# VectorE takes over one head of a third pair in 22 of 32 blocks of attention A

## The chip, the cores and the metric

The kernel runs as one program on one core of a Trainium2 chip. The metric is the device time of one execution in microseconds (us). The core has five engines with a queue each, and each works its queue strictly in order: TensorE (PE, with its weight loads shown as PEld), VectorE (DVE), ScalarE (ACT), GpSimd (POOL) and SyncE (SP), which here issues most transfers. They wait for one another through semaphores.

## The reference

Two independent attention problems over 2048 tokens and 576 features with 32 heads of 18 features, whose outputs stand side by side:

```python
# A: 32 query heads share one key head and one value head
q = (x @ wq).reshape(B, S, H, Dh).transpose(0, 2, 1, 3);  k = x @ wk;  v = x @ wv
p = softmax(einsum("bhqd,bkd->bhqk", q, k) * Dh ** -0.5)
a = einsum("bhqk,bkd->bhqd", p, v).transpose(0, 2, 1, 3).reshape(B, S, H * Dh) @ wo

# B: four segments of 512 tokens; in each, causal-like attention plus a memory of the segments before
logits = einsum("bhqd,bhkd->bhqk", qs, ks) * scale + mask
o = g * (phi(qs) @ M / den) + (1 - g) * (softmax(logits) @ vs)
M, z = M + phi(ks).T @ vs, z + phi(ks).sum()
```

What the change touches is A: for each head, 2048 x 2048 exponentials of scores, and their product with the values.

## The kernel before

**Stages.** In the first 290 us or so the projections, the key and value stacks and the bounds are made. Then comes the main stage, and at the end a last projection.

**Blocks.** The main stage is a list of blocks. A block of A is (c, hg): 512 queries (c = 0 to 3) and four heads (hg = 0 to 7), 32 blocks in all. Between them stand 32 small blocks of B, by a fixed list (`after`, line 874), mostly in pairs; from the fourth quarter of A on there are none left.

**Items.** A block of A has 16 key tiles `kt` of 128 keys. For each there are two items, `pr` 0 and 1, of two heads each: an item is one tile `E` of scores in PSUM, 128 keys x 2 heads x 512 queries. Its exponentials go to a tile `P` in SBUF, and `P` is multiplied with the values into `O`.

**Turns.** The program is written out in turns of three items. A block of A has 32 items, so eleven turns, 0 to 10, of which the last has two; a block of B has two turns. In turn k, TensorE makes the three `E` of this turn (line 924; line 932 for B), then one step of the output projection of an earlier quarter as "fill" (`F`, line 778; line 834 in the early blocks), then the products (`O`, line 972) that belong two turns back. ScalarE takes the exponentials (line 942) of the first and third item straight from PSUM. The middle item is first copied by VectorE to a tile `W` (line 939), which frees its PSUM early, and ScalarE takes it last. There are three tiles `E`, so each item of a turn waits for its counterpart of the turn before to be read: two for ScalarE, the middle one for VectorE's copy.

**The heads on VectorE.** For two items of each block of A, named in `BY_DVE` as (kt, pr), VectorE computes the exponentials of one of the two heads itself, and ScalarE only does the other: (0, 1) in turn 0 and (5, 0) in turn 3. Such a tile is named `PD` (two buffers). `exponentials` (line 896) first scales the scores from PSUM (line 900), and queues three pairs of operations, lines 902 and 903, 904 and 905, 906 and 907. One pair is worked off in each following turn (`slow`), behind this turn's copy. `copied` marks the middle item, so the copy to `W` shrinks to half where the item is also such an item.

**Positions of the products.** `turn_of` gives for each `pr` the order in which the key tiles are multiplied: the natural order, but the two tiles of `BY_DVE` are taken out and put in again at the positions `LATE` (7 and 12), since they are ready later.

**Other work on VectorE.** It copies finished `O` (line 981) and `F` (line 802) out of PSUM, and takes the reciprocals of the softmax sums (line 729): a large one for heads 0 to 27 of a quarter and a small one for heads 28 to 31. GpSimd multiplies finished heads with those inverses (line 762, "weighs"), behind the VectorE work of the same turn and only in a turn in which no pair is queued. In ten of the 32 blocks it does so.

The orders of TensorE, ScalarE and VectorE are as written in the program; those of GpSimd and SyncE are set by a scheduler.

Of the kernel before, what the change touches and what calls it, by code (L numbers as in the profile page):

```python
# [24 lines left out]
NKT = S // 128  # L25
# [26 lines left out]
POLY = [1.0925606709321247, 32.334180715292455, 88.7610992882796, 4291.093056129828]  # L52
MANTISSA, ONE_BITS, EXPONENT = 0x7FFFFF, 0x3F800000, 0xFF800000

BY_DVE = ((0, 1), (5, 0))
LATE = (7, 12)
QALL = [(slice(0, 36, 2), 0), (slice(1, 36, 2), 1), (slice(36, 54), 0)]
CA = 618
MZ = 126 + 32
# [15 lines left out]
def attention_pair_kernel(ctx, tc, a_xT, a_w, a_wo, b_xT, b_w, b_wo, b_beta, ident_d, hmask_d, bmask_d, cmask_d, sel_d, zmask_d, selx_d, sely_d, out):  # L75
# [534 lines left out]
    with tc.If(loose > 0, preferred_fallthrough_block=False):  # L610
        with ExitStack() as ph:
# [37 lines left out]
            with tc.For_i(0, H, 1) as h:  # L649
                qs = pq.tile([128, S], F32R, name="gq")  # L650
                load_rows(qs, qB, h, QALL)
                ks = pq.tile([128, S], F32R, name="gk")
                load_rows(ks, kB, h, KROWS)
                mc = pq.tile([128, 16], F32, name="gmc")
                for i in range(NKT):
                    s, j = divmod(i, 4)
                    n = 128 * (j + 1)
# [238 lines left out]
    def exponentials(p, e, whole):  # L896

        u, w = (pp.tile([128, 512], F32, name=nm, bufs=1) for nm in "nq")
        v, stt, y = nc.vector, nc.vector.scalar_tensor_tensor, p.bitcast(U32)
        v.tensor_scalar(y, e, EXP_A, EXP_B, op0=ALU.mult, op1=ALU.add)  # L900
        ops = [
            lambda: v.tensor_scalar(u.bitcast(U32), y, MANTISSA, ONE_BITS, op0=ALU.bitwise_and, op1=ALU.bitwise_or),
            lambda: v.tensor_scalar(w.bitcast(U32), y, EXPONENT, None, op0=ALU.bitwise_and),
            lambda: stt(p, u, POLY[0], u, op0=ALU.add, op1=ALU.mult),
            lambda: stt(p, p, POLY[1], u, op0=ALU.add, op1=ALU.mult),
            lambda: stt(p, p, POLY[2], p, op0=ALU.add, op1=ALU.mult),
            lambda: stt(p, p, POLY[3], w, op0=ALU.add, op1=ALU.mult),  # L907
        ]
        slow.extend((now[0] + 2 + i, p, ops[2 * i : 2 * i + 2], whole) for i in range(3))

    def scores(it, pr, copied):

        ab, c, hg, kt = it
        st = stacks[ab, c, hg // 2]
        h = 2 * (hg % 2) + pr
        e = psE.tile([128, 2, 512], F32, name="E")
        dve = ab == "A" and (kt, pr) in BY_DVE
        p = pp.tile([128, 2, 512], F32, name="PD" if dve else "P", bufs=2 if dve else PBUFS)
        state[it, pr] = p
        n = 512 if ab == "A" else 512 - 128 * kt if kt < 2 else 384  # L920
        if ab == "A":
            for j, r0 in enumerate(HALF):
                rows = slice(r0, r0 + KR)
                nc.tensor.matmul(e[:, j], kstA[rows, 128 * kt : 128 * kt + 128], st[rows, h, :], start=True, stop=True)  # L924
            if dve:
                exponentials(p[:, 0], e[:, 0], p)
        else:
            for k, c0 in BKEYS[kt]:
                ks = slice(128 * k, 128 * k + 128)
                for j, r0 in enumerate(HALF):  # L930
                    rows = slice(r0, r0 + KR)
                    nc.tensor.matmul(  # L932
                        e[:, j, c0 : c0 + 512 - 128 * k], st[rows, 4 + h, ks], st[rows, h, 128 * k :], start=True, stop=True
                    )
        src, hs = e, slice(0, 2)
        if copied:
            src = pp.tile([128, 2, 512], F32, name="W", bufs=2)
            hs = slice(1, 2) if dve else slice(0, 2)
            gate.append(nc.vector.tensor_copy(src[:, hs, :n], e[:, hs, :n]))  # L939

        def exponential():
            nc.scalar.activation(p[:, hs, :n], src[:, hs, :n], AF.Exp, scale=SCALE)  # L942
            if ab == "B":

                m = len(BKEYS[kt])
                diag = p.rearrange("p a (b t) -> p a b t", t=256)[:, :, 0:m, 0:128]
                nc.gpsimd.affine_select(  # L947
                    diag, diag, pattern=[[0, 2], [0, m], [1, 128]], base=0, channel_multiplier=-1, compare_op=ALU.is_ge, fill=0.0
                )

        return exponential
# [3 lines left out]
    def products(b, m, hf):  # L955


        ab, c, hg = b
        if m == hf == 0:
            acc[0] = psO.tile([128, C], F32, name="O")  # L960
        o = acc[0]
        last = (NKT - 1 if ab == "A" else 2) == m
        for j in range(4):
            kt = turn_of[j // 2][m] if ab == "A" else m
            p = state[b + (kt,), j // 2]
            assert all(x[3] is not p for x in slow)
            k, p0, q0, n = (kt, 256 * hf, 256 * hf, 256) if ab == "A" else BHALF[kt][hf]
            if ab == "A":
                v = VA[:, VW * kt : VW * kt + 32]
            else:  # L970
                v = vseg[c][:, k, VW * (4 * hg + j) : VW * (4 * hg + j) + 32]
            nc.tensor.matmul(  # L972
                o[32 * j : 32 * j + 32, q0 : q0 + n],
                v,
                p[:, j % 2, p0 : p0 + n],
                start=m == hf == 0,
                stop=last and hf == 1,
            )
        if last and hf:
            osb = pa.tile([128, C], F32, name="oe", bufs=4)  # L980
            nc.vector.tensor_copy(osb, o)  # L981
            od = oA if ab == "A" else oB
            nc.sync.dma_start(od[c][4 * hg : 4 * hg + 4].rearrange("h r t -> (h r) t"), osb)
            return hg
        return None


    turn_of = []
    for pr in range(2):
        ks = [kt for kt in range(NKT) if (kt, pr) not in BY_DVE]  # L990
        for (kt, p_), pos in zip(BY_DVE, LATE):
            if p_ == pr:
                ks.insert(pos, kt)
        turn_of.append(ks)

    keys = {ab: list(dict.fromkeys((ab, c, hg // 2) for a_, c, hg in blocks if a_ == ab)) for ab in "AB"}

# [94 lines left out]
    with tc.manual_schedule(engines={ENG.PE, ENG.Activation, ENG.DVE}):  # L1092
# [23 lines left out]
        for k in range(len(turns) + 2):  # L1116
            now[0] = k
            exps = [scores(its[n], pr, i == 1) for i, (n, pr) in enumerate(turns[k])] if k < len(turns) else []
            for i in (0, 2, 1) if len(exps) == 3 else range(len(exps)):
                exps[i]()  # L1120
# [148 lines left out]
```

## Time and profile before

| what | value |
|---|---|
| median of 3 runs | 1415.69 us (1415.11 to 1416.66) |
| the profiled execution's own time | 1417.1 us |
| its span, first to last instruction | 1415.4 us |
| granted TensorE clock, mean | 0.997 |
| main stage | from about 291 us to about 1376 us of the span |
| a block of A that follows a block of A, fourth quarter | 28.74 to 28.77 us |

The page gives for each engine the share of the span in which it is busy, and groups instructions by line, with the tile written and the tile read (`P<-E`). In the timeline every row is a start time, a duration, an engine, a line and a count of like instructions in a row; in square brackets stands how long the engine idled before it and what ended the wait. The duration of a ScalarE or VectorE row runs into the next row's start, since neighbours overlap; the distance from start to start tells what one instruction takes out of the engine's time. A view by windows gives, for stretches from one time to another, the length and the busy time of each engine in them. Cut at the starts of the `E` matmuls, such stretches are the turns.

### The profile page before, as it was taken

To read this page: it belongs to the slowest core of one execution; us is meant where nothing else is said; L and a number is where in the kernel's file an instruction comes from. 1 tells how busy PE (TensorE), PEld (TensorE's weight loads), DVE (VectorE), ACT (ScalarE), POOL (GpSimd) and SP (SyncE) were. 2 spreads that over 40 slices of the span, in tenths; PEclk is the share of its full clock that TensorE was granted. 3 is DMA by queue.
4 is the path that set the end of the run, shared out by engine and by line. 5 is a ranking of instruction groups with operands and counts; after the bars stand their busy time and mean duration, and the time that the engine had idled before them with its cause. 6 is when DMAs were issued, how large, how long until landed. Compare 5 with 4: busy or idle time off the path is not lost.

```text
span 1415.4 us, 40396 instructions
## 1 busy us (share of the span) xinstructions
PE 1397.0 (99%) x17132; PEld 843.5 (60%) x17132; DVE 976.6 (69%) x1413; ACT 1205.9 (85%) x1479; POOL 230.5 (16%) x326
## 2 busy tenths in 40 slices
PE   9999999989999999999999999999999999999998
PEld 6788888745554555555555555555555555555558
DVE  6656456466687767777777777766768777777763
ACT  4543434479999999999999999999999999999991
POOL 2431000003312310402110122113010320001002
PEclk9999999999999999999999999999999999999999
DMA  9766547466675445332312442232103321110013
GB/s 281 257 217 188 167 141 223 165 173 202 170 214 166 125 138 166 99 116 85 111 58 70 147 147 58 91 114 83 50 35 101 100 75 47 36 58 18 18 59 112
DMA packets 90723, 172.66 MB, mean 122 GB/s; under 512 B 14576, under 2 KB 22889, under 8 KB 90110
## 3 DMA queue, kind: packets, MB, share of 16 engines
q1 hardware_dynamic: 84122, 160.01, 36.8%
q0 software_dynamic: 1664, 4.78, 1.3%
q10 hardware_dynamic: 4752, 5.24, 1.1%
q8 instruction: 136, 2.23, 0.7%
q14 instruction: 49, 0.40, 0.1%
HBM read 99.32 MB, written 70.67 MB: 120 GB/s over the span
## 4 chain that ended last, share of the span: by engine, by line
PE 70%; ACT 4%; DMA 2%; DVE 2%; issue 1%; SPq 0%; ACTq 0%; DVEq 0%
PE O L972 32%; PE E L924 20%; PE F L778 11%; ACT P L942 4%; PE E L932 3%; PE E L1170 2%; DVE W L939 1%; PE F L834 1%; DMA vseg<-vB 0%; DMA stB<-qB 0%; DVE sm L729 0%; DMA woA<-a_wo 0%; DMA oA<-oe 0%; PE F L1170 0%; PE O L1170 0%
## 5 line engine op out<-in xcount | busy, mean ns | idle before, releaser
L942 ACT ACTIVATE P<-E 128x1024 f32<-128x1024 f32 (+1 forms) x800 | 804.8, 1116 | 3.1 <-PE E L924 2.9
L939 DVE COPY W<-E 128x1024 f32<-128x1024 f32 (+2 forms) x416 | 465.8, 1120 | 217.7 <-PE E L924 155.7
L972 PE MATMUL O<-P,VA 128*32 128x256 f32 x7680 | 508.1, 380 | 0.0
L942 ACT ACTIVATE P<-W 128x1024 f32<-128x1024 f32 (+1 forms) x352 | 410.4, 1166 | 5.3 <-DVE W L939 5.3
L972 PEld LDWEIGHTS O<-P,VA 128*32 128x32 f32 x7680 | 260.0, 110 | 139.1 <-issue 6.6
L924 PE MATMUL E<-stA,kstA 56*128 56x512 f32 x1920 | 321.6, 433 | 3.0 <-DVE W L939 2.0
L924 PEld LDWEIGHTS E<-stA,kstA 56*128 56x128 f32 x1920 | 154.9, 184 | 169.3 <-ACT P L942 77.8
L947 POOL TENSOR_SCALAR_AFFINE_SELECT P<-P 128x256 f32<-128x256 f32 (+1 forms) x192 | 94.5, 493 | 420.3 <-ACT P L942 381.8
L762 POOL TENSOR_TENSOR o<-o,rb 126x512 f32<-126x512 f32 (+1 forms) x55 | 72.6, 1350 | 480.4 <-DVE PD L907 377.3
L778 PE MATMUL F<-woB,o 126*32 126x192 f32 (+1 forms) x1920 | 127.0, 338 | 0.8 <-DVE osb L802 0.8
L778 PEld LDWEIGHTS F<-woB,o 126*32 126x32 f32 (+1 forms) x1920 | 38.5, 108 | 72.6 <-issue 66.7
L972 PE MATMUL O<-P,vseg 128*32 128x256 f32 (+2 forms) x1536 | 81.7, 344 | 0.0
L981 DVE COPY oe<-O 128x512 f32<-128x512 f32 x64 | 44.3, 692 | 42.0 <-PE O L972 41.1
L252 PE MATMUL pj<-xh,wBl 128*126 128x512 f32 x180 | 72.4, 403 | 0.0
L121 ACT CAST qp<-pj 126x512 fp32r<-126x512 f32 (+1 forms) x54 | 30.9, 585 | 48.2 <-DVE kmB L450 33.5
L252 PE MATMUL pj<-xh,wBh 128*126 128x512 f32 x180 | 71.8, 400 | 0.0
L972 PE MATMUL O<-PD,VA 128*32 128x256 f32 x512 | 71.8, 379 | 0.0
L932 PE MATMUL E<-stB 56*128 56x256 f32 (+3 forms) x512 | 62.4, 348 | 1.6 <-ACT P L942 0.9
L778 PE MATMUL F<-woA,o 126*32 126x192 f32 (+1 forms) x960 | 63.9, 338 | 0.0
L972 PEld LDWEIGHTS O<-P,vseg 128*32 128x32 f32 x1536 | 49.0, 109 | 24.5 <-issue 2.0
L900 DVE TENSOR_SCALAR PD<-E 128x512 uint32<-128x512 f32 x64 | 44.2, 691 | 27.3 <-PE E L924 26.5
L122 DVE TENSOR_TENSOR qp<-pj,qp 126x512 fp32r<-126x512 f32 (+1 forms) x54 | 36.7, 686 | 35.4 <-ACT qp L121 35.2
(195 smaller groups left out, 1485.0 us busy)
## 6 DMA issues: line engine op xcount, KB each, us to landing
stB<-kB SPq DMA_DIRECT2D x96, 144.0 KB
stB<-qB SPq DMA_DIRECT2D x32, 288.0 KB
stA<-qA SPq DMA_DIRECT2D x30, 288.0 KB
oA<-oe SPq DMA_DIRECT2D x32, 256.0 KB
oB<-oe SPq DMA_DIRECT2D x32, 256.0 KB
qA<-qp SPq DMA_DIRECT2D x16, 504.0 KB
kB<-qp SPq DMA_DIRECT2D x16, 504.0 KB
qB<-qp SPq DMA_DIRECT2D x16, 504.0 KB
```

The lines of the kernel that those rows point to most:

```text
L122: hold(nc.vector.tensor_tensor(qp[:R, 1, :n], src, qp[:R, 0, :n].bitcast(F32), op=ALU.subtract))
L252: nc.tensor.matmul(dst, w[:, c0 : c0 + M], x, start=i == 0, stop=i == len(ops) - 1)
L762: ins = tc.keep_in_program_order(nc.gpsimd.tensor_tensor(dst, a, b, op=op))
L778: nc.tensor.matmul(dst[32 * j : 32 * j + 32], parts[ab, c][: RT[t], t, r0 : r0 + 32], wo[ab][: RT[t], t, c0 : c0 + n], start=start, stop=stop,
L900: v.tensor_scalar(y, e, EXP_A, EXP_B, op0=ALU.mult, op1=ALU.add)
L924: nc.tensor.matmul(e[:, j], kstA[rows, 128 * kt : 128 * kt + 128], st[rows, h, :], start=True, stop=True)
L932: nc.tensor.matmul(e[:, j, c0 : c0 + 512 - 128 * k], st[rows, 4 + h, ks], st[rows, h, 128 * k :], start=True, stop=True)
L939: gate.append(nc.vector.tensor_copy(src[:, hs, :n], e[:, hs, :n]))
L942: nc.scalar.activation(p[:, hs, :n], src[:, hs, :n], AF.Exp, scale=SCALE)
L947: nc.gpsimd.affine_select(diag, diag, pattern=[[0, 2], [0, m], [1, 128]], base=0, channel_multiplier=-1, compare_op=ALU.is_ge, fill=0.0)
L972: nc.tensor.matmul(o[32 * j : 32 * j + 32, q0 : q0 + n], v, p[:, j % 2, p0 : p0 + n], start=m == hf == 0, stop=last and hf == 1,)
L981: nc.vector.tensor_copy(osb, o)
```

## The change

A third item, (9, 1), joins the table, in turn 6, but only in the blocks of A that are not in a new set `WEIGHED`: the ten blocks in which GpSimd weighs heads. So 22 blocks have three such items and ten have two. The table now holds the positions too: (0, 1) is multiplied at position 5, before at 7; (5, 0) stays at 12; (9, 1) stands at position 15, the last. `turn_of` becomes a function of the block.

```diff
-BY_DVE = ((0, 1), (5, 0))
-LATE = (7, 12)
+BY_DVE = {(0, 1): 5, (5, 0): 12, (9, 1): 15}
+WEIGHED = {(0, 3), (0, 6), (0, 7), (1, 1), (1, 6), (1, 7), (2, 2), (2, 6), (2, 7), (3, 4)}
...
-        dve = ab == "A" and (kt, pr) in BY_DVE
+        dve = ab == "A" and (kt, pr) in by_dve(c, hg)
         p = pp.tile([128, 2, 512], F32, name="PD" if dve else "P", bufs=2 if dve else PBUFS)
...
-            kt = turn_of[j // 2][m] if ab == "A" else m
+            kt = turn_of(c, hg)[j // 2][m] if ab == "A" else m
...
+    def by_dve(c, hg):
+
+        return [x for n, x in enumerate(BY_DVE) if n < 2 or (c, hg) not in WEIGHED]
+
+    def turn_of(c, hg):
+
+        order = []
+        for pr in range(2):
+            ks = [kt for kt in range(NKT) if (kt, pr) not in by_dve(c, hg)]
+            for kt, p_ in by_dve(c, hg):
+                if p_ == pr:
+                    ks.insert(BY_DVE[kt, p_], kt)
+            order.append(ks)
+        return order
```

VectorE's queue in block (3, 1) before, from the second pair of (5, 0) in turn 5 on; the copies belong to turns 6, 7, 8, 9 and 10:

```order
L904 SCALAR_TENSOR_TENSOR PD<-n 128x512
L905 SCALAR_TENSOR_TENSOR PD<-PD,n 128x512
L939 COPY W<-E 128x1024
L906 SCALAR_TENSOR_TENSOR PD<-PD 128x512
L907 SCALAR_TENSOR_TENSOR PD<-PD,q 128x512
L939 COPY W<-E 128x1024 x3
L802 COPY osb<-F 128x192
L939 COPY W<-E 128x1024
```

and with the change, from turn 6 on:

```order
L900 TENSOR_SCALAR PD<-E 128x512
L939 COPY W<-E 128x512
L906 SCALAR_TENSOR_TENSOR PD<-PD 128x512
L907 SCALAR_TENSOR_TENSOR PD<-PD,q 128x512
L939 COPY W<-E 128x1024
L902 TENSOR_SCALAR n<-PD 128x512
L903 TENSOR_SCALAR q<-PD 128x512
L939 COPY W<-E 128x1024
L904 SCALAR_TENSOR_TENSOR PD<-n 128x512
L905 SCALAR_TENSOR_TENSOR PD<-PD,n 128x512
L939 COPY W<-E 128x1024
L802 COPY osb<-F 128x192
```

The whole copy of turn 6 has become a scaling and a half copy, and a pair stands behind the copy of each of the turns 7, 8 and 9 (the last of the three pairs follows the row shown last).

VectorE's queue in block (0, 5), one of the three blocks of A (hg = 5 in quarters 0 to 2) in which the largest reciprocal is taken, before, from the copy of turn 6 on:

```order
L939 COPY W<-E 128x1024
L802 COPY osb<-F 128x192
L906 SCALAR_TENSOR_TENSOR PD<-PD 128x512
L907 SCALAR_TENSOR_TENSOR PD<-PD,q 128x512
L729 RECIPROCAL sm_6557<-sm_6557 112x256
L732 TENSOR_SCALAR sm_6557<-sm_6557,omg 112x128
L939 COPY W<-E 128x1024 x3
L729 RECIPROCAL sm_6638<-sm_6638 128x32
```

and with the change, from the reciprocal on:

```order
L729 RECIPROCAL sm_6593<-sm_6593 112x256
L732 TENSOR_SCALAR sm_6593<-sm_6593,omg 112x128
L939 COPY W<-E 128x1024
L902 TENSOR_SCALAR n<-PD 128x512
L903 TENSOR_SCALAR q<-PD 128x512
L939 COPY W<-E 128x1024
L904 SCALAR_TENSOR_TENSOR PD<-n 128x512
L905 SCALAR_TENSOR_TENSOR PD<-PD,n 128x512
L939 COPY W<-E 128x1024
L906 SCALAR_TENSOR_TENSOR PD<-PD 128x512
L907 SCALAR_TENSOR_TENSOR PD<-PD,q 128x512
L729 RECIPROCAL sm_6674<-sm_6674 128x32
```

The three pairs stand between the two reciprocals, where there were only copies.

TensorE's queue in block (3, 1) before, turns 5 and 6 (`E` scores, `F` fill, `O` products; `PD` where the product reads a tile with a head from VectorE):

```order
L924 MATMUL E<-stA,kstA 128x512 x6
L778 MATMUL F<-woA,o 32x192 x4
L972 MATMUL O<-P,VA 32x256 x12
L924 MATMUL E<-stA,kstA 128x512 x6
L778 MATMUL F<-woA,o 32x192 x4
L972 MATMUL O<-P,VA 32x256 x10
L972 MATMUL O<-PD,VA 32x256 x2
```

and with the change:

```order
L924 MATMUL E<-stA,kstA 128x512 x6
L778 MATMUL F<-woA,o 32x192 x4
L972 MATMUL O<-P,VA 32x256 x6
L972 MATMUL O<-PD,VA 32x256 x2
L972 MATMUL O<-P,VA 32x256 x2
L972 MATMUL O<-PD,VA 32x256 x2
L924 MATMUL E<-stA,kstA 128x512 x6
L778 MATMUL F<-woA,o 32x192 x4
L972 MATMUL O<-P,VA 32x256 x12
```

The product of (0, 1) has moved from turns 6 and 7 into turn 5, all of it ahead of the `E` of turn 6. The number of matmuls in a turn is the same.

More of the change, by code (lines that the diff above doesn't have):

```diff
@@ L985, in products @@
         return None
[L988 to L994, printed above, removed]
+    def by_dve(c, hg):
[9 more added lines that the diff above has]
+        return order
     keys = {ab: list(dict.fromkeys((ab, c, hg // 2) for a_, c, hg in blocks if a_ == ab)) for ab in "AB"}
```

## The prediction

> **What bounds the kernel now.** I read the page first, then the main stage turn by turn.
>
> ```profile
> PE 1397.0 (99%) x17132; PEld 843.5 (60%) x17132; DVE 976.6 (69%) x1413; ACT 1205.9 (85%) x1479; POOL 230.5 (16%) x326
> ACT  4543434479999999999999999999999999999991
> ```
>
> TensorE reads 99% busy, but ScalarE is at nine tenths or more in every slice of the main stage too. Both cannot be told apart from shares, so I cut one block of A that follows a block of A, (3, 1), at the starts of its `E` matmuls. Each row is a turn: its length, then busy time by engine. These are turns 0, 1, 7, 8, 9 and 10, and the sum of all eleven.
>
> ```profile
> 1168.82:1171.04 2.22, 2.22 (x34) 1.16 (x30) 1.44 (x3) 2.22 (x3) 0.00 (x0) 1.00 0.02 7
> 1171.04:1173.82 2.78, 2.78 (x44) 1.43 (x40) 1.74 (x3) 2.78 (x5) 0.00 (x0) 1.00 0.00 0
> ...
> 1187.06:1189.71 2.65, 2.65 (x43) 1.42 (x39) 1.93 (x3) 2.65 (x4) 0.00 (x0) 1.00 0.00 0
> 1189.71:1192.38 2.67, 2.67 (x42) 1.42 (x38) 1.23 (x1) 2.67 (x4) 0.00 (x0) 1.00 0.00 0
> 1192.38:1195.16 2.78, 2.78 (x42) 1.42 (x38) 1.49 (x2) 2.78 (x4) 0.00 (x0) 1.00 0.00 0
> 1195.16:1197.58 2.42, 2.42 (x42) 1.24 (x38) 1.23 (x1) 2.42 (x4) 0.00 (x0) 1.00 0.55 159
> sum 28.76, PE 28.76 PEld 15.18 DVE 21.32 ACT 28.76 POOL 0.00; mean PE 2.61 PEld 1.38 DVE 1.94 ACT 2.61 POOL 0.00
> ```
>
> Turns of the same matmuls take 2.65 us in the middle of the block and 2.78 at turns 1 and 9. (Turn 0 has fewer products, turn 10 fewer scores.) ScalarE has no idle time in any of them. What differs is who makes TensorE wait:
>
> ```profile
> 1187.06 0.56 PEld L924 LDWEIGHTS E<-stA,kstA 56*128 56x128 f32 x6 [0.41 <-issue]
> ...
> 1192.98 0.19 PEld L924 LDWEIGHTS E<-stA,kstA 56*128 56x128 f32 x2 [0.30 <-ACT P L942]
> ```
>
> In turn 7 TensorE loads its six weights in one go; in turn 9 the last two stand 0.30 us until ScalarE has read the third `E` of the turn before. So 2.65 is TensorE's own pace, and 2.78 is ScalarE's. ScalarE's pace shows in the timeline of (3, 0):
>
> ```profile
> 1148.65 2.08 ACT L942 ACTIVATE P<-E 128x1024 f32<-128x1024 f32 x2
> 1150.45 0.79 ACT L942 ACTIVATE PD<-W 128x512 f32<-128x512 f32 x1
> 1150.98 2.10 ACT L942 ACTIVATE P<-E 128x1024 f32<-128x1024 f32 x2
> ...
> 1153.75 2.10 ACT L942 ACTIVATE P<-E 128x1024 f32<-128x1024 f32 x2
> ```
>
> From start to start, a turn with a half item takes it 1150.98 - 1148.65 = 2.33 us, a full turn 1153.75 - 1150.98 = 2.77. It loses 0.12 on TensorE in every full turn, wins it back in turns 0, 3 and 10, and by turn 8 its delay reaches TensorE. Over a block the two engines are nearly level: ScalarE needs all of 28.76 us, TensorE 2.22 + 2.42 + 9 x 2.65 = 28.49.
>
> **ScalarE's half.** In 22 blocks a whole item of turn 6 becomes a half: 2.77 - 2.33 = 0.44 us less ScalarE work each. TensorE's pace caps what of it is seen. From turn 7 on the delay is 0.44 smaller, more than the 0.02, 0.13 and 0.13 by which turns 8, 9 and the next block's turn 1 exceed 2.65, so all three go: 0.28 per block. ScalarE then has 28.32 us of work against 28.49 and idles. Nine of the 22 blocks are followed by another block of A and meet no large reciprocal; the sum of eight of them stands here, and the last block of A is the ninth.
>
> ```profile
> sum 229.87, PE 229.87 PEld 121.94 DVE 172.08 ACT 229.81 POOL 2.49; mean PE 28.73 PEld 15.24 DVE 21.51 ACT 28.73 POOL 0.31
> ```
>
> 9 x 0.28 = 2.5 us; bounds 0 (the 2.78s are something else) and 9 x 0.44 = 4.0 (TensorE could go faster).
>
> Seven more blocks are followed by a pair of blocks of B. There the delay is also seen in B's second turn:
>
> ```profile
> 940.06:942.86 2.80, 2.80 (x47) 1.65 (x43) 0.96 (x1) 2.80 (x5) 1.49 (x4) 1.00 0.01 3
> ...
> 940.50 0.53 PEld L932 LDWEIGHTS E<-stB 56*128 56x128 f32 x8 [0.25 <-ACT P L942]
> ```
>
> The 0.15 of turns 8 and 9 goes as before. Of the 0.25 here I take 0.21: with the whole 0.44 gone, ScalarE would be ahead of VectorE's copy of turn 10 and wait for that instead. 7 x 0.36 = 2.5, bounds 7 x 0.15 = 1.05 and 7 x 0.40 = 2.8.
>
> The first block, (0, 0), has no fill. These are the starts of turns 5, 6, 8 and 9:
>
> ```profile
> 305.19 0.96 PE L924 MATMUL E<-st,kstA 56*128 56x512 f32 x6
> 307.52 1.21 PE L924 MATMUL E<-st,kstA 56*128 56x512 f32 x6
> ...
> 312.87 0.72 PE L924 MATMUL E<-st,kstA 56*128 56x512 f32 x4
> ...
> 315.64 0.72 PE L924 MATMUL E<-st,kstA 56*128 56x512 f32 x4
> ```
>
> TensorE can do a turn there in 2.33 and is held at 2.77, so all 0.44 counts (bounds 0 and 0.44). In (0, 1) and (0, 2) the fill is wider (line 834) and I credit nothing, 0.44 each at most.
>
> **VectorE's side.** What its operations take:
>
> ```profile
> 1148.49 0.69 DVE L900 TENSOR_SCALAR PD<-E 128x512 uint32<-128x512 f32 x1
> 1149.10 0.68 DVE L939 COPY W<-E 128x512 f32<-128x512 f32 x1
> 1149.70 0.68 DVE L906 SCALAR_TENSOR_TENSOR PD<-PD 128x512 f32<-128x512 f32 x1
> 1150.41 0.69 DVE L907 SCALAR_TENSOR_TENSOR PD<-PD,q 128x512 f32<-128x512 f32 x1
> 1151.21 1.23 DVE L939 COPY W<-E 128x1024 f32<-128x1024 f32 x1
> 1152.36 0.42 DVE L902 TENSOR_SCALAR n<-PD 128x512 uint32<-128x512 uint32 x1
> 1152.69 0.42 DVE L903 TENSOR_SCALAR q<-PD 128x512 uint32<-128x512 uint32 x1
> ...
> 1155.00 0.35 DVE L802 COPY osb<-F 128x192 f32<-128x192 f32 x1
> 1155.27 0.68 DVE L904 SCALAR_TENSOR_TENSOR PD<-n 128x512 f32<-128x512 f32 x1
> 1155.98 0.69 DVE L905 SCALAR_TENSOR_TENSOR PD<-PD,n 128x512 f32<-128x512 f32 x1
> 1156.60 1.22 DVE L939 COPY W<-E 128x1024 f32<-128x1024 f32 x1
> ...
> 1161.80 1.23 DVE L939 COPY W<-E 128x1024 f32<-128x1024 f32 x1 [1.42 <-PE E L924]
> ```
>
> By starts: scaling 0.61, half copy 0.60, whole copy 1.15, first pair 0.33 + 0.42 = 0.75, second 0.71 + 0.62 = 1.33, third 0.71 + 0.69 = 1.40. Turn 6 was 1.15 + 1.40 = 2.55 and becomes 0.61 + 0.60 + 1.40 = 2.61; turns 7, 8 and 9 were a copy alone (the 1.42 idle ahead of turn 8's) and become 1.90, 2.48 and 2.55. That is 3.54 us more per block, 78 us in all, and every turn still ends inside 2.65. The cover is that idle time. Where an evacuation (0.27) joins turn 9, the next copy is 2.82 - 2.65 = 0.17 late. ScalarE takes that copy last in its turn, and the 0.17 us it idles per block after the change (28.49 - 28.32) pay for it. So nothing in ordinary blocks; bounds 0 and 0.17 x 16 = 2.7.
>
> A rule of the Trainium skill (VectorE: DVE Perf Modes, section "The DRAIN you can't avoid") speaks against this: the next operation starts only when the pipeline of the one before is empty. By it turns 6 and 9 would cost their full durations, 2.74 and 2.60, with an evacuation 2.95, and some 0.15 more per ordinary block would come off, 2.4 us in all, leaving 1.2 of the gain. The rows disagree: the operation behind the half copy starts 0.60 after it though it lasts 0.68.
>
> Where a large reciprocal stands in the queue, the idle time is already used up (block (0, 5)):
>
> ```profile
> 533.26 1.75 DVE L729 RECIPROCAL sm<-sm 112x256 f32<-112x256 f32 x1
> ...
> 535.24 2.35 DVE L939 COPY W<-E 128x1024 f32<-128x1024 f32 x2
> ...
> 536.51 0.50 PE L924 MATMUL E<-stA,kstA 56*128 56x512 f32 x2 [0.54 <-DVE W L939]
> ```
>
> Here turn 7's copy already waits for the reciprocal and TensorE for the copy. ScalarE idles too, so its 0.44 buys nothing. Turn 6's extra 0.06 lengthens that wait. Behind it, turn 8's copy moves by the first pair, 0.75, and turn 10's by what the idle time no longer absorbs, about half a microsecond, of which I let 0.2 reach TensorE. So 3 blocks x 0.25 = 0.75 lost; bounds 3 x 0.06 and 3 x 1.40, the last pair in full.
>
> Block (0, 2) has smaller reciprocals but the wide fill, whose evacuations (line 839) load VectorE as well:
>
> ```profile
> 413.90 1.23 DVE L939 COPY W<-E 128x1024 f32<-128x1024 f32 x1 [1.63 <-PE E L924]
> 415.04 0.74 DVE L839 TENSOR_SCALAR o<-F,gt 126x512 f32<-126x512 f32 x1
> 415.70 0.24 DVE L729 RECIPROCAL sm<-sm 128x16 f32<-128x16 f32 x1
> ```
>
> Turns 7 to 9 get 0.75 + 1.33 + 1.40 = 3.48 against 1.63 of idle time ahead of turn 9's copy and 0.4 or so behind it: turn 10's copy comes about 1.3 late, and I book 1.1 (bounds 0.4 and 1.4).
>
> **Costed at nothing.** The product of (0, 1) moves from turns 6 and 7 to 5; its last pair is done in turn 3, and it must be out before the scaling of (9, 1) takes its buffer in turn 6, which it is by a whole `E` group. Its tiles 9 to 15 are multiplied one position earlier; the tightest, ScalarE's last item of a turn, is read second in the next turn's products, as other tiles are already before. The stores of the small inverses on SP's queue move behind one or two loads in four places; their readers are issued turns later. GpSimd's queue keeps its order, and the weighing blocks get no third head.
>
> **The sum.** Gains 2.5 + 2.5 + 0.44 = 5.4; costs 0.75 + 1.1 = 1.85; net 3.6 us. The profiled execution took 1417.1 (span 1415.4) and would take 1413.5; the median of the runs is 1.4 below it, so I forecast 1412.1, 0.25% less. A measurement tells about 0.2%, 2.8 us, from no change.
>
> **Rivals.** *The bubbles stay.* Turn 1 and B's second turn follow a short turn 0, and a short turn may simply be less than one round trip from `E` through ScalarE back to TensorE, whatever the delay. For it: both follow the 2.22 turn. Against: ScalarE has no idle time there. Then only turns 8 and 9 give, 16 x 0.15 = 2.4, plus 0.44, less 1.85: 1.0 us, 1414.7.
>
> *VectorE ends last* (slower). Place: the copies of turns 8 to 10. It decides once a copy stands more than the 0.17 a block can spare behind. For it: four turns in a row now fill 2.48 to 2.61 of 2.65. Against: turn 6 is 2.55 before and does not hold TensorE up. If pairs took 0.3 more each, turns 8 and 9 would be 2.78 and 2.85 where they were 2.67 and 2.78: 0.18 x 16 blocks = 2.9, plus 1.85 and no gain: 1420.
>
> *ScalarE alone is the bound.* If TensorE's 2.65 were not its floor, the whole 22 x 0.44 = 9.7 would go: 1406. For it: ScalarE never idles. Against: turn 7, where TensorE does not wait, is no shorter than 2.65. The Trainium skill (Perfetto Trace Analysis, section "Identifying the Most-Contended Engine") says to disregard matmul busy time and to take the busiest of the others, which by the page's 85% is ScalarE; that is this rival.
>
> **Chances and range.** Forecast 0.60, bubbles stay 0.25, VectorE last 0.11, ScalarE alone 0.04. The net of the forecast spreads from 2 to 6 us by its bounds, about five in six of it above 2.8. Faster by over 0.2%: 0.50 + 0.04 = 0.54; within: 0.10 + 0.25 = 0.35; slower: 0.11. The range goes from all gains without costs (5.9 with B's upper bound, 1409.7, and a little for (0, 1)) to just above no change: 1409.2 to 1416.5; the forecast's own is 1409.7 to 1413.7.
>
> **What would show it.** Turns 8 and 9 at 2.65 in the 16 ordinary blocks, turn 1 near 2.65, idle time on ScalarE once per block, VectorE busy some 78 us more, longer waits for line 939 in the hg = 5 blocks. Turns of 2.8 from turn 8 on with waits for line 939 everywhere would make it wrong, as would a turn 1 still at 2.78.

## The result, and the profile after

| | median of the runs | ratio to before, 95% interval | (0, 1) to (3, 7), us |
|---|---|---|---|
| before | 1415.71 us (22 runs) | | 1001.79 |
| changed | 1412.83 us (22 runs) | 0.9983 [0.9977, 0.9990] | 998.79 |

The changed kernel is 0.17% faster, 2.4 us by the ratio; 1412.1 was forecast. The last column is the stretch of the profiled execution from the first scores of block (0, 1) to those of the last block, (3, 7). It leaves out two places that differ between executions of one kernel, and will serve as the finer measure. One run of those told below, with a half left out, took 1890.48 us at a granted clock of 0.654, and its ratio does not count it.

From the page of the changed kernel, busy time and ScalarE's slices:

```profile
PE 1393.8 (99%) x17132; PEld 846.7 (60%) x17132; DVE 1046.6 (74%) x1567; ACT 1198.1 (85%) x1479; POOL 230.1 (16%) x326
ACT  4543434479999999999999999999999999999991
```

VectorE has 70.0 us more to do (976.6 before), ScalarE 7.8 less (1205.9 before). Block (3, 1) by turns (length, then busy time of PE, PEld, DVE and ACT), turns 0, 1, 8, 9 and 10 and the sum:

```profile
1167.15:1169.37 2.22, 2.22 (x34) 1.16 (x30) 1.45 (x3) 2.22 (x3) 0.00 (x0) 1.00 0.07 26
1169.37:1172.03 2.66, 2.66 (x44) 1.43 (x40) 1.73 (x3) 2.66 (x5) 0.00 (x0) 1.00 0.00 0
...
1187.92:1190.56 2.64, 2.64 (x42) 1.42 (x38) 1.89 (x3) 2.64 (x4) 0.00 (x0) 1.00 0.00 0
1190.56:1193.21 2.65, 2.65 (x42) 1.42 (x39) 2.52 (x5) 2.65 (x5) 0.00 (x0) 1.00 0.03 6
1193.21:1195.62 2.41, 2.41 (x40) 1.24 (x36) 2.11 (x3) 2.27 (x4) 0.00 (x0) 1.00 0.56 159
sum 28.47, PE 28.47 PEld 15.21 DVE 24.55 ACT 28.33 POOL 0.00; mean PE 2.59 PEld 1.38 DVE 2.23 ACT 2.58 POOL 0.00
```

Turns 1 and 9 have gone from 2.78 to 2.66 and 2.65: the block lasts as long as TensorE needs, and ScalarE idles 0.14 us in turn 10. What it waits for there is seen in VectorE's queue from turn 9 into the next block, and in ScalarE's:

```profile
1191.40 1.23 DVE L939 COPY W<-E 128x1024 f32<-128x1024 f32 x1
1192.54 0.35 DVE L802 COPY osb<-F 128x192 f32<-128x192 f32 x1
1192.81 0.68 DVE L906 SCALAR_TENSOR_TENSOR PD<-PD 128x512 f32<-128x512 f32 x1
1193.52 0.69 DVE L907 SCALAR_TENSOR_TENSOR PD<-PD,q 128x512 f32<-128x512 f32 x1
1194.13 1.22 DVE L939 COPY W<-E 128x1024 f32<-128x1024 f32 x1
1196.39 0.69 DVE L900 TENSOR_SCALAR PD<-E 128x512 uint32<-128x512 f32 x1 [1.04 <-PE E L924]
```

```profile
1194.15 1.10 ACT L942 ACTIVATE P<-E 128x1024 f32<-128x1024 f32 x1
1195.38 1.06 ACT L942 ACTIVATE P<-W 128x1024 f32<-128x1024 f32 x1
```

VectorE works without a gap from turn 9 into turn 10. The copy ends at 1194.13 + 1.22 = 1195.35, and ScalarE takes it at 1195.38, with nothing to do in between. So VectorE, though idle 1.04 us right behind, is at that one place already last.

Where the change costs, in (0, 2), the same queue runs past the end of the block:

```profile
415.95 0.68 DVE L906 SCALAR_TENSOR_TENSOR PD<-PD 128x512 f32<-128x512 f32 x1
416.66 0.69 DVE L907 SCALAR_TENSOR_TENSOR PD<-PD,q 128x512 f32<-128x512 f32 x1
417.27 0.25 DVE L729 RECIPROCAL sm<-sm 128x16 f32<-128x16 f32 x1
417.55 0.24 DVE L732 TENSOR_SCALAR sm<-sm,omg 128x16 f32<-128x16 f32 x1
417.70 1.22 DVE L939 COPY W<-E 128x1024 f32<-128x1024 f32 x1
```

```profile
418.97 0.19 PEld L932 LDWEIGHTS E<-stB 56*128 56x128 f32 x2 [0.36 <-DVE W L939]
```

The copy of turn 10 ends 0.6 us into block B (1, 0); TensorE waits for it and, later in that block, for ScalarE. The block of B lasts 5.40 us where it lasted 4.46. In (0, 5), behind the large reciprocal, TensorE waits longer for the copy than before (0.54):

```profile
537.04 0.49 PE L924 MATMUL E<-stA,kstA 56*128 56x512 f32 x2 [0.78 <-DVE W L939]
```

But it only comes to this wait sooner. From the start of the block the wait ends after 537.04 - 514.74 = 22.30 us, before after 536.51 - 514.18 = 22.33, and turn 8 takes 3.70 in both.

### The profile page after: what moved, and what is told of

Same layout as the page of the kernel before. It is cut to its first block, busy times and chain, and to the rows that moved or that the text cites. A ratio compares the mean times of both kernels' runs of the same rounds, so it can differ in the third digit from the quotient of the medians.

```text
span 1411.0 us, 40566 instructions
## 1 busy us (share of the span) xinstructions
PE 1393.8 (99%) x17132; PEld 846.7 (60%) x17132; DVE 1046.6 (74%) x1567; ACT 1198.1 (85%) x1479; POOL 230.1 (16%) x326
## 4 chain that ended last, share of the span: by engine, by line
PE 71%; ACT 4%; DVE 2%; issue 1%; DMA 1%; SPq 0%; POOL 0%; ACTq 0%
PE O L972 33%; PE E L924 20%; PE F L778 11%; ACT P L942 4%; PE E L932 3%; PE E L1178 2%; DVE W L939 1%; PE F L834 1%; DMA vseg<-vB 0%; DVE sm L729 0%; DMA woA<-a_wo 0%; PE F L1178 0%; PE O L1178 0%; DVE o L839 0%; DVE oe L981 0%
## 5 line engine op out<-in xcount | busy, mean ns | idle before, releaser
L942 ACT ACTIVATE P<-E 128x1024 f32<-128x1024 f32 (+1 forms) x800 | 786.8, 1073 | 3.0 <-PE E L924 2.7
L939 DVE COPY W<-E 128x1024 f32<-128x1024 f32 (+2 forms) x416 | 453.7, 1091 | 142.7 <-PE E L924 82.0
L942 ACT ACTIVATE P<-W 128x1024 f32<-128x1024 f32 (+1 forms) x330 | 369.4, 1119 | 7.4 <-DVE W L939 6.7
L924 PE MATMUL E<-stA,kstA 56*128 56x512 f32 x1920 | 317.3, 430 | 3.1 <-DVE W L939 2.1
L972 PE MATMUL O<-PD,VA 128*32 128x256 f32 x688 | 88.9, 379 | 0.0
L900 DVE TENSOR_SCALAR PD<-E 128x512 uint32<-128x512 f32 x86 | 59.4, 691 | 26.5 <-PE E L924 25.0
```

Source lines behind the costliest of these rows:

```text
L972: nc.tensor.matmul(o[32 * j : 32 * j + 32, q0 : q0 + n], v, p[:, j % 2, p0 : p0 + n], start=m == hf == 0, stop=last and hf == 1,)
```

## The experiments

Each run is told by its difference from the changed kernel. First all of them, with the stretch from (0, 1) to (3, 7) in their profiled executions (before: 1001.79):

| run | median, us | ratio to before, 95% interval | stretch, us |
|---|---|---|---|
| position alone | 1414.89 | 0.9998 [0.9988, 1.0007] | 1001.78 |
| no relief for ScalarE | 1418.46 | 1.0020 [1.0011, 1.0029] | 1002.91 |
| half left out | 1409.23 | 0.9951 [0.9939, 0.9964] | 995.16 |
| item left out | 1407.92 | 0.9939 [0.9924, 0.9953] | 993.78 |
| not in the four | 1411.55 | 0.9968 [0.9955, 0.9981] | 997.20 |
| lighter four | 1409.44 | 0.9956 [0.9944, 0.9968] | 995.26 |
| split reciprocal | 1408.71 | 0.9947 [0.9933, 0.9961] | 994.39 |
| dearer pair, turn 9 | 1426.07 | 1.0069 [1.0056, 1.0083] | 1009.60 |
| a little dearer, turn 9 | 1417.14 | 1.0006 [0.9997, 1.0015] | 1002.60 |
| dearer pair, turn 7 | 1416.45 | 1.0001 [0.9992, 1.0010] | 1001.16 |
| all 32 blocks | 1431.59 | 1.0107 [1.0092, 1.0122] | 1017.44 |
| changed, again | 1413.81 | 0.9979 [0.9970, 0.9988] | 998.89 |

### Which part makes the gain

**Position alone.**

```diff
-WEIGHED = {(0, 3), (0, 6), (0, 7), (1, 1), (1, 6), (1, 7), (2, 2), (2, 6), (2, 7), (3, 4)}
+WEIGHED = {(c, hg) for c in range(4) for hg in range(8)}
```

> The product of (0, 1) at position 5 instead of 7 in all blocks, and no third head anywhere. Theory (the relief of ScalarE makes the gain): no change, 1415.7, within 0.4; block (3, 1) at 28.76 with 2.78 in turns 1 and 9. Rival (the earlier position makes the gain, by giving the buffer of the head back sooner): a part of the 2.9 us is there already, 1413 to 1415.

No change: the stretch is that of before to 0.01 us, and turns 1 and 9 of (3, 1) are 2.77. The moved product costs and brings nothing.

**No relief for ScalarE.**

```diff
-        state[it, pr] = p
+        state[it, pr] = (p, p)
+        if dve and (kt, pr) == (9, 1):
+            twice = pp.tile([128, 2, 512], F32, name="P", bufs=PBUFS)
+            state[it, pr] = (p, twice)
...
-            nc.scalar.activation(p[:, hs, :n], src[:, hs, :n], AF.Exp, scale=SCALE)
+            if dve and (kt, pr) == (9, 1):
+                nc.scalar.activation(twice[:, :, :n], src[:, hs, :n].to_broadcast([128, 2, n]), AF.Exp, scale=SCALE)
+            else:
+                nc.scalar.activation(p[:, hs, :n], src[:, hs, :n], AF.Exp, scale=SCALE)
...
-            p = state[b + (kt,), j // 2]
+            p = state[b + (kt,), j // 2][j % 2]
```

> VectorE does the third head as in the changed kernel, but ScalarE still exponentiates 1024 columns for that item (the 512 of the other head twice, into another buffer whose second half is what the products read), so only VectorE's added work and its shorter copy are left of the change. Theory (ScalarE and TensorE set the pace, VectorE's idle time covers its work): ordinary blocks stay as before, (3, 1) about 28.76 with VectorE near 24.5 us of it busy; the four blocks cost what they cost in the changed kernel, 1.5, and up to 0.17 x 16 = 2.7 where a late copy is no longer paid for by ScalarE's idle time: 1417.2, up to 1419.9. Rival (VectorE ends last): turns 8 and 9 at 2.78 and 2.85, (3, 1) near 28.95, 1420 or more.

Block (3, 1), turns 1, 8, 9 and 10 and the sum:

```profile
1171.33:1174.10 2.77, 2.77 (x42) 1.42 (x38) 1.74 (x3) 2.77 (x5) 0.00 (x0) 1.00 0.00 0
...
1190.01:1192.66 2.65, 2.65 (x42) 1.41 (x39) 1.90 (x3) 2.65 (x4) 0.00 (x0) 1.00 0.00 0
1192.66:1195.43 2.77, 2.77 (x43) 1.42 (x40) 2.63 (x5) 2.77 (x4) 0.00 (x0) 1.00 0.02 6
1195.43:1197.86 2.43, 2.43 (x41) 1.23 (x38) 2.04 (x3) 2.43 (x4) 0.00 (x0) 1.00 0.52 149
sum 28.74, PE 28.74 PEld 15.17 DVE 24.61 ACT 28.74 POOL 0.00; mean PE 2.61 PEld 1.38 DVE 2.24 ACT 2.61 POOL 0.00
```

VectorE's work is that of the changed kernel (24.61), the turns and ScalarE are those of before (28.74). So the third head's operations alone neither win nor lose in such a block, and the 2.77s are ScalarE's delay. Two of the 16 ordinary blocks do get longer, (2, 1) by 0.13 and (3, 2) by 0.11. Of the 1.12 by which the stretch is longer, 1.03 lies in (0, 2) with the block of B behind it. The runs say 2.8 (1.6 to 4.1); the rest lies outside the stretch or was absent from the one profiled execution, the fastest of the eleven. It stays open.

**Half left out**, and then, with the first lines of the same edit, the whole item.

```diff
-            if dve:
+            if dve and (kt, pr) != (9, 1):
                 exponentials(p[:, 0], e[:, 0], p)
...
-                p[:, j % 2, p0 : p0 + n],
+                p[:, 1 if ab == "A" and (kt, j // 2) == (9, 1) and (9, 1) in by_dve(c, hg) else j % 2, p0 : p0 + n],
```

> The exponentials of the third head are left out altogether in the 22 blocks: its products read the other head's weights in their place, VectorE gets no third pair, and ScalarE has its half item as in the changed kernel. Theory (TensorE's 28.49 us per block is the floor): the gains of the change without its costs, 5 to 5.4 us less than before, 1410.3 to 1410.7; block (3, 1) at 28.47 as in the changed kernel, ScalarE idle 0.15 to 0.2 in it. Rival (ScalarE alone is the bound, and VectorE's work took the rest): 22 x 0.44 = 9.7 us, 1406, and (3, 1) near 28.32.

```diff
+        if dve and (kt, pr) == (9, 1):
+            return lambda: None
         if copied:
...
-            p = state[b + (kt,), j // 2]
+            p = state[b + (15 if ab == "A" and (kt, j // 2) == (9, 1) and (9, 1) in by_dve(c, hg) else kt,), j // 2]
```

> In the 22 blocks the whole item of the third head is left out behind its scores: no exponentials on either engine, no copy; its products read another item's weights, and TensorE's work is unchanged. ScalarE loses about 0.93 us per block against the kernel before, not 0.44, and VectorE has less work than before. Theory (TensorE's 28.49 us per block is the floor): ordinary blocks stay at 28.47 to 28.49 as with half the item left out; more comes only from the four blocks where a copy behind a reciprocal holds TensorE up, at most 1 us each beside what the half brought: 1407 to 1409. Rival (ScalarE's work sets the pace, and TensorE could go faster): 22 x 0.93 = 20 us less than before, 1395; block (3, 1) near 27.8.

Block (3, 1) with the half left out, and with the item left out:

```profile
sum 28.48, PE 28.48 PEld 15.17 DVE 20.79 ACT 28.41 POOL 0.00; mean PE 2.59 PEld 1.38 DVE 1.89 ACT 2.58 POOL 0.00
```

```profile
sum 28.49, PE 28.49 PEld 15.17 DVE 20.19 ACT 28.01 POOL 0.00; mean PE 2.59 PEld 1.38 DVE 1.84 ACT 2.55 POOL 0.00
```

With ScalarE at 28.41 or 28.01 and VectorE far below both, the block stays at the changed kernel's 28.47 to 28.49. That is TensorE's floor, and the rival "ScalarE alone" (27.8) is out. But the half left out won 1.1 to 1.5 us more than expected: (0, 2), (0, 5), (1, 5) and (2, 5), where nothing was looked for, became 0.32, 0.51, 0.52 and 0.54 shorter than before. In these four VectorE's queue is the bound, and a half copy in place of a whole one takes some 0.55 us out of it. ScalarE's relief can't be the reason, since the changed kernel has the same, and none of the four is shorter there by more than 0.02.

### The four blocks

**Not in the four.**

```diff
-WEIGHED = {(0, 3), (0, 6), (0, 7), (1, 1), (1, 6), (1, 7), (2, 2), (2, 6), (2, 7), (3, 4)}
+WEIGHED = {(0, 3), (0, 6), (0, 7), (1, 1), (1, 6), (1, 7), (2, 2), (2, 6), (2, 7), (3, 4), (0, 2), (0, 5), (1, 5), (2, 5)}
```

> The third head is left out in four more blocks, (0, 2), (0, 5), (1, 5) and (2, 5); the other 18 keep it. If the cost of the change lies in these four blocks alone (local theory), their lengths go back to those of the kernel before, which by the two traces is 1.03 + 0.00 + 0.20 + 0.26 = 1.5 us less than in the changed kernel, and all else stays: 1412.8 - 1.5 = 1411.3, ratio to before about 0.997, turn 8 of (2, 5) at 3.43 again. Rival: the delay of (0, 2) and of the reciprocals is made good or lost elsewhere whatever these blocks do (a stage that starts later, a transfer that sets the end): then no more than 0.3 us changes, 1412.5 to 1412.8.

The stretch is 1.59 us shorter than in the changed kernel, as forecast. B (1, 0), 5.40 us long there, is back at 4.45, and (2, 5) at 29.59. The cost of the change is local, and the third head is worth having elsewhere.

**Lighter four.** The second head, too, is taken from VectorE there (`WEIGHED` as in the run before).

```diff
+LIGHT = {(0, 2), (0, 5), (1, 5), (2, 5)}
...
-        return [x for n, x in enumerate(BY_DVE) if n < 2 or (c, hg) not in WEIGHED]
+        return [x for n, x in enumerate(BY_DVE) if n == 0 or (c, hg) not in LIGHT and (n == 1 or (c, hg) not in WEIGHED)]
```

> No third head in the four blocks, and their second head, (5, 0), goes back to ScalarE too: VectorE has 3.5 us less to do there than in the kernel before, 1.40 of it straight ahead of the reciprocals, and ScalarE 0.44 more. Theory (in these four blocks VectorE's queue, reciprocal and copies, is the bound, and ScalarE idles behind it): turn 8 of (0, 5), (1, 5) and (2, 5) falls from 3.70, 3.44 and 3.44 to 2.8 to 2.9, that of (0, 2) from 3.12 to 2.77; less 0.1 to 0.2 each where ScalarE's 0.44 shows: 1.5 to 2.5 us less than with the third head left out there, 1409 to 1410. Rival (ScalarE is the bound there as well): 4 x 0.44 = 1.8 us longer than that, 1413.3.

VectorE's queue in (0, 5), around the reciprocal:

```profile
528.26 1.22 DVE L940 COPY W<-E 128x1024 f32<-128x1024 f32 x1 [1.53 <-PE E L925]
529.40 0.35 DVE L803 COPY osb<-F 128x192 f32<-128x192 f32 x1
529.67 1.74 DVE L730 RECIPROCAL sm<-sm 112x256 f32<-112x256 f32 x1
531.44 0.29 DVE L733 TENSOR_SCALAR sm<-sm,omg 112x128 f32<-112x128 f32 x1
531.65 1.22 DVE L940 COPY W<-E 128x1024 f32<-128x1024 f32 x1
```

Less work for VectorE and more for ScalarE, the reverse of the change, and 1.94 us less in the stretch than with the third head merely left out. Turn 8 falls to 3.01, 2.77 and 2.78, (0, 2) by 0.31. Now turns 5 to 9 of (2, 5) are 2.74 to 2.78, ScalarE's pace.

**Split reciprocal.** The second head stays in the hg = 5 blocks, and their reciprocal is cut in two and comes a turn later (in (0, 2) the second head goes back to ScalarE, as in the run before).

```diff
...
-            at(k + d1, 0, lambda: True, inv)
+            if ab == "B" and c > 0 and hg == 6:
+                at(k + d1 + 1, 0, lambda: True, first)
+            else:
+                at(k + d1, 0, lambda: True, inv)
+
+        def first(k):
+            inverses(ab, c, lo, hi, box[0], 0)
+            at(k + 1, 0, lambda: True, lambda k: inv(k, 1))
...
```

> As the run with no third head in the four blocks, but in (0, 2) the second head goes back to ScalarE too, and in (0, 5), (1, 5) and (2, 5) the large reciprocal is cut into two of 112x128, one in turn 7 and one in turn 8, a turn after the last pair of the second head. Theory (these blocks are long because one turn of VectorE's holds pair, reciprocal and copy together): turn 7 becomes 1.15 + 0.27 + 0.94 + 0.28 = 2.64 us of work and turn 8 less, so nothing is late, and the three blocks come to 28.75 to 28.9 from 29.85, 29.58 and 29.58; with 0.3 in (0, 2) some 2.8 us less than 1411.5: 1408.7. Rival (the inverses, a turn later, hold up the weighing or the output projection behind them): what is gained is lost in the blocks behind, 1410 to 1412.

(0, 5), turn 7 and the start of turn 8:

```profile
531.14 1.21 DVE L945 COPY W<-E 128x1024 f32<-128x1024 f32 x1
532.28 0.94 DVE L735 RECIPROCAL sm<-sm 112x128 f32<-112x128 f32 x1
533.25 0.29 DVE L738 TENSOR_SCALAR sm<-sm,omg 112x128 f32<-112x128 f32 x1
533.72 1.22 DVE L945 COPY W<-E 128x1024 f32<-128x1024 f32 x1 [0.18 <-PE E L930]
```

Turn 7's copy, which TensorE waited for before, is no longer late. (1, 5) and (2, 5) take 28.68, a little less than expected. (0, 5) takes 29.03: in its turn 9 four of TensorE's six weight loads stand 0.40 us until ScalarE has read, where in (1, 5) and (2, 5) only the last two do, for 0.29. The small reciprocal and the second half meet in turn 8 in all three blocks, so that is not the reason; why (0, 5) differs was not found. The run changes two things at once, the cut and the later turn, and does not tell them apart. At 1408.71 us, 0.53% below before, this is the fastest complete version, and 4.40 us below the changed kernel in the stretch.

### How much room VectorE has

**Dearer pair in turn 9.**

```diff
+        if third:
+            ops.insert(5, lambda: stt(u, p, POLY[3], w, op0=ALU.add, op1=ALU.mult))
-        slow.extend((now[0] + 2 + i, p, ops[2 * i : 2 * i + 2], whole) for i in range(3))
+        slow.extend((now[0] + 2 + i, p, ops[2 * i : 2 * i + 2 + (i == 2)], whole) for i in range(3))
...
```

Here and in the next runs `third` is true for the item (9, 1).

> The changed kernel with one operation more in the third head's last pair (a scalar_tensor_tensor of 128x512 into a buffer that is free): turn 9 has three of 0.70, 2.55 + 0.70 = 3.25 us of VectorE's work against a turn of 2.65, so 0.60 hang over. Theory (only idle time of the block as a whole counts, and turn 10 has 1.2 of it before the copy that ScalarE reads last in its turn): no more than 0.2 per block, 1412.8 to 1416. Rival (VectorE ends last as soon as one turn overflows): 16 x 0.60 = 9.6 us at least, 1422 or more, turns 9 and 10 longer by 0.6 together.

The theory was wrong here and the rival nearer: 10.8 us more than the changed kernel in the stretch. TensorE's weight loads in turns 0 and 1 of (3, 2), behind (3, 1):

```profile
1202.57 0.30 PEld L926 LDWEIGHTS E<-stA,kstA 56*128 56x128 f32 x4 [0.41 <-DMA stA<-qA]
1203.08 0.19 PEld L926 LDWEIGHTS E<-stA,kstA 56*128 56x128 f32 x2 [0.21 <-DVE W L941]
1203.51 0.16 PEld L778 LDWEIGHTS F<-woA,o 126*32 126x32 f32 x8 [0.24 <-issue]
1205.08 0.30 PEld L926 LDWEIGHTS E<-stA,kstA 56*128 56x128 f32 x4 [0.66 <-ACT P L944]
```

Turns 8 to 10 of the block keep 2.64, 2.65 and 2.41. The overrun comes out behind the border, 2.51 and 3.11 for turns 0 and 1: the late copies first hold up TensorE itself (0.21), then ScalarE, for which TensorE waits 0.66.

**A little dearer in turn 9.**

```diff
...
+            few = slice(0, 128)
+            pairs[2].insert(1, lambda: stt(u[:, few], p[:, few], POLY[3], w[:, few], op0=ALU.add, op1=ALU.mult))
```

> The changed kernel with a small operation more in the third head's last pair in turn 9 (a scalar_tensor_tensor of 128x128 where the run with the dearer pair had 128x512, some 0.2 us to the next start by the durations of the 128x192 and 128x512 operations). In that run 0.70 more cost about 0.5 at the border to the next block, and nothing within the block. Theory (the border has some 0.2 of slack, and only what exceeds it counts): 0 to 0.1 per block, 1412.8 to 1415; block (3, 1) within 0.1 of 28.47, and turn 1 of the next block at 2.65 to 2.75. Rival (no slack is left, each addition counts in full): 16 x 0.2 = 3.2 us at least, 1416 or more.

The operation took 0.32 from start to start, and turn 1 of block (3, 2) is again late:

```profile
1196.32 0.29 DVE L912 SCALAR_TENSOR_TENSOR n<-PD,q 128x128 f32<-128x128 f32 x1
1196.64 0.69 DVE L907 SCALAR_TENSOR_TENSOR PD<-PD,q 128x512 f32<-128x512 f32 x1
```

```profile
1200.64:1203.63 2.99, 2.91 (x43) 1.42 (x40) 1.73 (x3) 2.99 (x5) 0.00 (x0) 1.00 0.55 129
```

Block (3, 2), behind a turn 9 with an evacuation, grew by 0.31, the operation's whole length; (3, 1), behind a turn 9 without one, by 0.10. So the slack at the border is about zero in the one case and 0.2 in the other (0.32 less 0.10), and the changed kernel stands just at the edge. The runs (1417.14) are on the rival's side.

**The same dearer pair in turn 7.**

```diff
+        pairs = [ops[:2], ops[2:4], ops[4:]]
+        if third:
+            pairs[0].append(ops[2])
-        slow.extend((now[0] + 2 + i, p, ops[2 * i : 2 * i + 2], whole) for i in range(3))
+        slow.extend((now[0] + 2 + i, p, pairs[i], whole) for i in range(3))
...
```

> The same extra operation as in the run with the dearer pair, 128x512 and about 0.70 us, as often and in the same blocks, but in the third head's first pair, in turn 7, which then has 1.90 + 0.70 = 2.60 us of work against 2.65. Theory (the place decides: what fits into its turn is free): as the changed kernel, 1412.8, within 1, block (3, 1) at 28.5; a cost of up to 1 only behind the reciprocals of the four blocks. Rival (VectorE's work as such sets the end, wherever it stands): the 13.2 us of the dearer pair in turn 9 again, 1426.

Block (3, 1), turn 8, into which VectorE's queue carries the extra operation, and the sum:

```profile
1190.55:1193.19 2.64, 2.64 (x42) 1.41 (x38) 2.58 (x4) 2.64 (x4) 0.00 (x0) 1.00 0.00 0
...
sum 28.47, PE 28.47 PEld 15.16 DVE 25.22 ACT 28.36 POOL 0.00; mean PE 2.59 PEld 1.38 DVE 2.29 ACT 2.58 POOL 0.00
```

VectorE has 25.22 us to do, as with the dearer pair in turn 9 (25.23), and the block is at its floor. So in an ordinary block it is the place that decides. The price behind the reciprocals was underestimated: 2.4 us in the stretch, most of it in (0, 2), (0, 5) and (1, 5) with the blocks behind them.

### All 32 blocks

```diff
-WEIGHED = {(0, 3), (0, 6), (0, 7), (1, 1), (1, 6), (1, 7), (2, 2), (2, 6), (2, 7), (3, 4)}
+WEIGHED = set()
...
-        slow.extend((now[0] + 2 + i, p, ops[2 * i : 2 * i + 2], whole) for i in range(3))
+        slow.extend((now[0] + 2 + i, p, ops[2 * i : 2 * i + 2], whole, third) for i in range(3))
...
-        heavy *= "B" not in near and not slow
+        heavy *= "B" not in near and not [x for x in slow if not x[4]]
```

> The third head in all 32 blocks, the ten in which GpSimd weighs heads too (GpSimd's weighing is let go ahead while only the third head's pairs are queued, as otherwise it comes too late). Theory (a half item less on ScalarE is worth what exceeds TensorE's 28.49, wherever VectorE is idle for it): the ten blocks stand 0.25 to 0.3 above 28.49 and give it back, 2.5 to 2.8 us, 1410.2. Rival (VectorE and GpSimd disturb one another there): VectorE's operations get longer in these blocks than in the others, their turns rise to 2.8 or more, and the time is that of the changed kernel or longer, 1413 to 1416.

The rival held, and by more than it said: 18.65 us longer than the changed kernel in the stretch. VectorE and GpSimd in (3, 4):

```profile
1289.76 0.65 DVE L902 TENSOR_SCALAR n<-PD 128x512 uint32<-128x512 uint32 x1
1290.33 1.51 DVE L903 TENSOR_SCALAR q<-PD 128x512 uint32<-128x512 uint32 x1
1291.76 1.21 DVE L939 COPY W<-E 128x1024 f32<-128x1024 f32 x1
1292.89 0.85 DVE L904 SCALAR_TENSOR_TENSOR PD<-n 128x512 f32<-128x512 f32 x1
1293.79 1.66 DVE L905 SCALAR_TENSOR_TENSOR PD<-PD,n 128x512 f32<-128x512 f32 x1
```

```profile
1288.84 2.72 POOL L762 TENSOR_TENSOR o<-o,rb 126x512 f32<-126x512 f32 x2 [134.07 <-DVE PD L907]
1291.92 2.98 POOL L762 TENSOR_TENSOR o<-o,rb 126x512 f32<-126x512 f32 x2 [0.36 <-DVE q L903]
```

While GpSimd weighs, a 0.42 us operation takes 1.51 and a 0.69 one 1.66; the copy out of PSUM keeps its 1.21. The second and third pair no longer fit, and turn 10 of (3, 4) takes 3.17. The loss lies in the ten blocks and those right behind them: turn 0 of (3, 0), behind (2, 7), takes 4.26 for 2.21. A third head in these ten blocks, with the weighing beside it, costs six times what it brings in the other 22. Weighing moved elsewhere was not tried.

### Once more

> The changed kernel itself, once more, for a second profile of it. In its first profile turn 5 of the last block (3, 7) took 2.65 us, in that of the kernel before 3.82, because the large reciprocal there waited 1.21 us for the transfer of its input; in the other runs turn 5 stands between 2.65 and 4.28. Theory (this wait varies from execution to execution, or belongs to the end of every version, and is no part of the change): the stretch from the start of (0, 1) to that of (3, 7) is again 998.8 us, within 0.1, and turn 5 of (3, 7) is likely 3.8 to 4.3. Rival (the change takes this wait away, 1.2 us of the gain): 2.65 again. The time does not tell them apart: 1412.8 either way.

The stretch is 998.89, within 0.1. The reciprocal in turn 5 of (3, 7), in the first profile of the changed kernel and in this one:

```profile
1349.37 0.94 DVE L729 RECIPROCAL sm<-sm 112x128 f32<-112x128 f32 x1
```

```profile
1350.42 0.95 DVE L729 RECIPROCAL sm<-sm 112x128 f32<-112x128 f32 x1 [1.65 <-DMA sm<-oA]
```

The turn takes 2.65 in the one and 4.27 in the other: this wait is no part of the change.

## Why the prediction was right, point by point

Differences of the two first profiles, added up by the prediction's steps:

| step | predicted, us | measured, us |
|---|---|---|
| turns 8 and 9 of the 16 blocks, and turn 1 of the blocks of A behind nine of them | -3.57 (9 x 0.28 + 7 x 0.15) | -3.40 |
| second turn of seven pairs of B | -1.47 (7 x 0.21) | -1.16 |
| (0, 0), turns 8 and 9 | -0.44 | -0.36 |
| (0, 2) and B (1, 0) | +1.1 | +1.02 |
| blocks with the large reciprocal, and behind | +0.75 | +0.36 |
| sum | -3.6 | -3.5 |

The last of the nine is the last block of A, with no turn 1 behind it, so one 0.13 of the first step could not come. The gains came out 0.56 smaller than predicted and the costs 0.47 smaller: that the sums agree to 0.1 is in part luck.

- **TensorE's floor caps ScalarE's half.** Right, and shown: 28.47 to 28.49 with ScalarE at 28.33, 28.41 and 28.01. The Trainium skill (Perfetto Trace Analysis, section "Identifying the Most-Contended Engine") disregards matmul busy time; by it ScalarE was the engine to relieve. The trace agrees only down to that floor: the last 0.4 us taken off ScalarE brought nothing in these blocks.
- **The bubbles are ScalarE's delay.** Right: they stay without its relief and go with it. The 2.75 to 2.76 left in turn 1 of (2, 0), (3, 0) and (3, 5) stand behind blocks without a third head. In (1, 0), behind another such block, turn 1 even rose, from 2.76 to 2.88 and 2.87 in the two profiles; why was not found.
- **B's second turn.** Right in kind, too large: 0.11 to 0.20 instead of 0.21.
- **VectorE hidden in ordinary blocks.** Right (70 us more busy time, where the text's 78 counts from start to start), and closer to the edge than the text let it seem. It had the copy behind turn 9 late by 0.17 where an evacuation joins, paid for by ScalarE's idle time. The rows show the kind and half the size: from copy to copy turn 9 takes VectorE 1194.13 - 1191.40 = 2.73, 0.08 over 2.65, ScalarE's idle time is a wait for that copy, and 0.32 us more came out as 0.31. Three turns are nearly full, not "four turns in a row": by the text's own sums turn 7 holds 1.90 of 2.65.
- **The DRAIN rule.** By full durations 1.2 of the gain would be left, and neither gains nor rows bear that out: turn 9 with an evacuation takes VectorE 2.73, not 2.95. The section of the Trainium skill that the prediction took the rule from (VectorE: DVE Perf Modes, section "The DRAIN you can't avoid") adds that an operation which is not held starts earlier, and the prediction left that half out.
- **(0, 2).** Right, 1.02 for 1.1, and by the mechanism named: turn 10's copy late.
- **Large reciprocals.** Right in sign, half in size, and only in part by the step named: nothing in (0, 5), 0.19 behind (1, 5), 0.26 in (2, 5). The last begins ahead of the reciprocal and of the third head. These are the copies of turn 5 of (2, 5), before and with the change:

```profile
1066.68 1.23 DVE L939 COPY W<-E 128x1024 f32<-128x1024 f32 x1 [0.70 <-PE E L924]
```

```profile
1065.33 1.23 DVE L939 COPY W<-E 128x1024 f32<-128x1024 f32 x1 [1.06 <-ACT P L942]
```

Before, this copy starts 0.84 us into its turn, with the change 1.20, since it waits for ScalarE, and the queue behind it is full up to the copy that TensorE waits for. The same wait stands in the second profile of the changed kernel and in the run with no relief, where turn 8 takes 3.66 and 3.68, and in no other run. Four of the others have the third head in this block too (all 32, both dearer in turn 9, dearer in turn 7), and turn 8 takes 3.43 to 3.45 there. So the third head's pairs are not what makes it. Why the copy waits for ScalarE in these three was not found.
- **"Its 0.44 buys nothing" in these blocks.** Right as the change stands. Its sum for turn 6 (0.61 + 0.60 for 1.15) holds a part that is worth much by itself: the half copy relieves VectorE, 0.5 per block in (0, 5), (1, 5) and (2, 5) with the half left out, and the scaling beside it takes 0.61 back.
- **Time and sum.** The profiles' sum is the forecast's to 0.1 us, the runs show 2.4 and, again, 3.0 less by their ratios. At 0.17% the change falls just inside the 0.2% that the prediction set as the least it could tell from no change; to that outcome it gave 0.35. The 5.9 at the upper end of its gains is 5.7 by its own terms (2.5 + 2.8 + 0.44). The missing 0.5 to 1.1 us was not located. It may lie where executions of one kernel differ by more than that: at the start of the stage, and in the wait in (3, 7).

## What to carry to other kernels

When two engines are level, shave the later one only down to the other's floor, and read that floor from turns in which it does not wait. Work moved to a third engine is free turn by turn, not by its idle share: in ordinary blocks 0.70 us cost nothing in turn 7 and half a microsecond or more in turn 9, just ahead of a copy that is taken last. And look at each block for who is last there: in four of 32 even the opposite move paid, and a long operation cut in two and moved a turn on brought 0.8 to 0.9 us in each of three.

## What the hardware showed

GpSimd's tensor_tensor between buffers in SBUF held up VectorE's operations in SBUF, from 0.42 and 0.69 us to 1.51 and 1.66, but not its copies out of PSUM (1.21). The Trainium skill (SBUF — State Buffer, section "Who interferes with whom") says that the two engines share one pair of ports, which one of them holds alone, and of VectorE's two-port modes that whoever issues first has it for the whole instruction; the trace agrees in kind.

Two profiled executions of one kernel agreed to 0.1 us over 999 us of the main stage, while their last block differed by 1.6 us in one turn. A small change is better read from the stage than from the end to end time.
